# Moving the on-chip tiles of an attention and two-block MLP kernel to other byte positions within 128

## The chip, the cores and the metric

The kernel runs on one core of a Trainium2 chip. The time is the device time in microseconds of one execution; the time before is the median of three runs. A profile is one further execution, taken with the hardware profiler on.

In the profile PE is the matrix engine's matmuls, PEld its weight loads, DVE the vector engine, ACT the scalar engine, POOL the GpSimd engine and SP the engine whose queue issues all DMAs here.

## The reference

Three stages follow each other. Attention runs over 2 batches, 8 heads, 576 positions and a head width of 64; of each row of scores only the 32 largest count. Its output, 1152 rows of 512, goes through a first block (weights `moe_w_in` 512 x 2048 and `moe_w_out` 2048 x 512, Mish between them) and a second one of the same sizes with SiLU.

```python
scores = scale * np.matmul(q, k.transpose(0, 1, 3, 2))
kth = np.partition(scores, -top_k, axis=-1)[..., -top_k:-top_k + 1]
scores = np.where(scores >= kth, scores, -1e9)          # then softmax, then times v
h = x @ w_in;  g = h * np.tanh(softplus(h));  x = g @ w_out      # first block
h = x @ w_in;  g = h / (1 + np.exp(-h));      return g @ w_out   # second block
```

## The kernel before, in words

The 1152 rows are nine tiles of 128. `attention` (from line 356) works on one tile and one pair of heads at a time: scores on PE (line 391), copies to the tile `sc`, four rounds of finding and striking out the eight largest on DVE (lines 407 and 410), the exponential on ACT, transposes on PE (line 452, `e` against the identity matrix), the product with `v` (lines 468 and 471), and the result into the row tile `xt`.

`block1` (line 659) and `block2` (line 779) take the row tiles in groups, listed in `BLOCK1` and `BLOCK2`. A group marked `n` holds one 128-row tile (in the second block's first group two) and multiplies in plain fp32; each such matmul stands in the profile as two MATMUL records. A group marked `r` holds two tiles, 256 rows, and multiplies in the fp32r format: each operand is split into a high and a low part and three products are summed (`passes`, line 605), one record each. In the input products (line 644) the weights are the stationary operand, which PEld loads, and the rows (`xt` in the first block, `y` in the second) are the moving operand that streams through PE. In the first block's output product (line 714) the weights are stationary and the activations (`hs` in plain groups, `g` in split ones) move. In the second block's output product (line 821) it is the other way: `th` or `g` is stationary, and the weights move, 512 columns at a time. Weights lie in the tiles `wraw` (plain), `ws` (split) and `keep` (split, held for all groups).

The class `Plan` orders all steps by ranks and costs written in the tables at the top, and then emits them; each engine runs its instructions in that order.

All tiles in on-chip memory come from one pool, `sb`, through the helper `sbuf(tag, shape)`: a tag's first call reserves its buffers side by side, at the next multiple of 32 bytes of each partition. Tags follow each other in the order of their first calls, so a tile's length sets where the following ones lie. What this gives in the built program, as the byte position within 128 (the same in all 128 partitions, and for every slice that a matmul reads, since those slices begin at multiples of 128 bytes within their tiles):

| tiles | before |
|---|---|
| `ident` | 0 |
| `qraw`, `kraw` | 64 |
| `wide`, three buffers | 64, 96, 0 |
| `v`, `qs`, `kk`, `wraw`, `sc`, `ws`, `m8`, `rest` | 32 |
| `bias`, `den` (16 bytes each, at 32-byte steps) | all four |
| `e`, `x`, `pt`, `dt`, `xt`, `hs`, `y`, `th`, `g`, `o`, `keep` | 96 |

Of the kernel before, what the change touches and what calls it, by code (L numbers as in the profile page):

```python
# [10 lines left out]
F32 = mybir.dt.float32  # L11
F32R = mybir.dt.float32r
I32 = mybir.dt.int32
U32 = mybir.dt.uint32
I16 = mybir.dt.int16
# [5 lines left out]
P = 128  # L21
TOPK = 32
UNIT = 512
ONE16 = 2.0 ** 19
FAR = 2.0 ** 80
LOWEST = -3.0e38
# [46 lines left out]
class Plan:  # L73
# [13 lines left out]
    def add(self, ways, reads=(), writes=(), uses=(), rank=0.0, boost=0.0, table=None, load=0.0):  # L87

        first = rank - (boost if not isinstance(boost, str) else OFF[boost])
        offset = lambda o: o if not isinstance(o, str) else FLEX1[o] if rank < EARLY and o in FLEX1 else FLEX[o]
        ways = [(w[0], w[1], offset(w[2]), w[3], w[4] if len(w) > 4 else w[0] == "pool") for w in ways
                if offset(w[2]) is not None]
        self.steps.append(dict(ways=ways, reads=reads, writes=writes, uses=uses, rank=rank, first=first, table=table, load=load))
# [140 lines left out]
def act_us(n, psum=False):  # L237
    return (0.051 if psum else 0.093) + n * 0.000833


def dve_us(n):
    return 0.07 + n * 0.00104
# [6 lines left out]
def pool_us(n):  # L249
    return 0.18 + n * 0.0021  # L250
# [3 lines left out]
def kernel(ctx: ExitStack, tc, qh, kh, va, w1i, w1o, w2i, w2o, out):  # L254
# [11 lines left out]
    wide = {"w1i": w1i, "w1o": w1o, "w2i": w2i, "w2o": w2o}  # L266

    sb = ctx.enter_context(tc.tile_pool(name="sb", bufs=1))
    ps = ctx.enter_context(tc.tile_pool(name="ps", bufs=1, space=PSUM))
    dp = ctx.enter_context(tc.tile_pool(name="dp", bufs=1, space=DRAM))  # L270

    def sbuf(tag, shape, dtype=F32):
        return sb.tile(shape, dtype, tag=tag, name=tag, bufs=SBUF_BUFS.get(tag, KEEP))

    def psum(tag, shape):
        return ps.tile(shape, F32, tag="ps_" + tag, name="ps_" + tag, bufs=PSUM_BUFS[tag])
# [9 lines left out]
    def get(key, make):  # L286
        if key not in T:
            T[key] = make()
        return T[key]
# [18 lines left out]

    ident = sb.tile([P, P], F32, name="ident", bufs=1)
    make_identity(nc, ident)  # L310
    zone = sb.tile([P, 1], F32, name="zone", bufs=1)
    nc.gpsimd.memset(zone, -ONE16 * 14336)
    tiny = sb.tile([P, 1], F32, name="tiny", bufs=1)
    nc.gpsimd.memset(tiny, 1e-9)


# [2 lines left out]
    def load_kv(b, p, rank):  # L319
        if (b, p) in kv_done:  # L320
            return
        kv_done.add((b, p))
        kk, vv = ("kk", b, p), ("v", b, p)
        raw = ("kraw", b, p)
        first = b == 0 and p == 0
        for h in ([0], [1]) if first else ([0, 1],):
            hs = slice(h[0], h[-1] + 1)
            add([("sp", 0.06, 0, lambda hs=hs: nc.sync.dma_start(
                out=get(raw, lambda: sbuf("kraw", [P, 2, S]))[:, hs], in_=kh[b, p][:, hs]))],
                writes=[raw + (i,) for i in h], uses=[(raw, "kraw")], rank=rank - 8, boost="kload", load=len(h) * P * S * 4)  # L330
        for h in range(2):
            hi = lambda h=h: get(kk, lambda: sbuf("kk", [P, 2, S], F32R))[:, h]
            lo = lambda h=h: T[kk][D:, h]
            src = lambda h=h: T[raw][:, h]
            U = [(raw, "kraw"), (kk, "kk")]
            add(copy_ways(S, hi, src, dve="khi", twice=True), reads=[raw + (h,)], writes=[kk + (h, 0)], uses=U,
                rank=rank - 6, boost="k")
            add(tt_ways(S, lo, lambda h=h: T[raw][D:, h], lo, ALU.subtract, dve="klo"), reads=[raw + (h,), kk + (h, 0)], writes=[kk + (h, 1)],
                uses=U, rank=rank - 6, boost="k")
        add([("sp", 0.06, 0, lambda: nc.sync.dma_start(out=get(vv, lambda: sbuf("v", [P, NB + 1, D])), in_=va[b, p]))],  # L340
            writes=[vv], uses=[(vv, "v")], rank=rank, load=P * (NB + 1) * D * 4)
# [14 lines left out]
    def attention(t, p, rank):  # L356
# [8 lines left out]
        K = lambda name, *rest: (name,) + key + rest  # L365
# [36 lines left out]
        for i in range(TOPK // 8):  # L402
            for h in range(2):
# [5 lines left out]
                if i < TOPK // 8 - 1:  # L409
# [1 line left out]
                        out=rest()[:, h], in_to_replace=m8()[:, h, 8 * i:8 * i + 8], in_values=src()[:, h], imm_value=LOWEST))],  # L411
                        reads=srck + [K("m8", h, i)], writes=[K("rest", h)],
                        uses=srcu + [(K("rest"), "rest"), (K("m8"), "m8")] if i == 0 else srcu + [(K("m8"), "m8")], rank=rank)
        bias = lambda: get(K("bias"), lambda: sbuf("bias", [P, 2, 2, 1]))
        den = lambda: get(K("den"), lambda: sbuf("den", [P, 2, 2, 1]))
        for i, (col, by) in enumerate([(TOPK - 1, FAR), (0, -scale)]):
            if i == 0 and t < MASK:
                continue
# [86 lines left out]
    def convert(name, src, dst, rank, four):  # L505
        wk, sk, gk = ("w",) + name, ("pn",) + name, ("wide",) + name

        def fetch():
            t = get(gk, lambda: sbuf("wide", [P, 2 * UNIT + 2], I32)).bitcast(I16)[:, 1:1 + 4 * UNIT]
            s = src.bitcast(I16)  # L510
            if four:
                t = t.rearrange("p (f j) -> p f j", f=4)
            nc.sync.dma_start(out=t, in_=s)
        add([("sp", 0.06, 0, fetch)], writes=[gk], uses=[(gk, "wide")], rank=rank - 10, boost="cload", load=P * UNIT * 8)
        pn = lambda: get(sk, lambda: sbuf("ws", [P, 2, UNIT], I32))
        top = lambda: T[gk].bitcast(I16)[:, 4:4 + 4 * UNIT].rearrange("p (n t) -> p n t", t=4)[:, :, 0]
        mid = lambda: T[gk].bitcast(U32)[:, 1:1 + 2 * UNIT].rearrange("p (n t) -> p n t", t=2)[:, :, 0]
        for i in range(2):
            add([("act", act_us(UNIT) + 0.14, 0, lambda i=i: nc.scalar.activation(  # L519
                pn()[:, i], top(), AF.Relu, scale=ONE16 - 2 * ONE16 * i, bias=zone))],  # L520
                reads=[gk], writes=[sk + (i,)], uses=[(gk, "wide"), (sk, "ws")], rank=rank - 5, boost="cpn")
        se = lambda: pn()[:, 0]
        ways = [("pool", pool_us(UNIT), 0, lambda: nc.gpsimd.tensor_tensor(out=se(), in0=pn()[:, 0], in1=pn()[:, 1],  # L523
                                                                           op=ALU.subtract))]
        ways.append(("dve", dve_us(UNIT), "se", lambda: nc.vector.tensor_tensor(
            out=se(), in0=pn()[:, 0], in1=pn()[:, 1], op=ALU.subtract), True))
        add(ways, reads=[sk + (1,)], writes=[sk + (0,)], uses=[(sk, "ws")], rank=rank - 3, boost="cse")
        w = lambda: get(wk, lambda: sbuf("wraw", [P, UNIT]))
        T["conv"] = T.get("conv", 0) + 1
        if ADD and T["conv"] % ADD == 0:  # L530
            add([("act", act_us(UNIT) + 0.05, 0, lambda: nc.scalar.activation(w().bitcast(I32), mid(), AF.Copy, scale=2.0 ** -13))],  # L531
                reads=[gk], writes=[wk], uses=[(gk, "wide"), (wk, "wraw")], rank=rank - 5, boost="cmid")
            add([("pool", pool_us(UNIT), 0, lambda: nc.gpsimd.tensor_tensor(out=w().bitcast(I32), in0=w().bitcast(I32), in1=se(),  # L533
                                                                            op=ALU.add))],
                reads=[wk, sk + (0,)], writes=[wk], uses=[(sk, "ws"), (wk, "wraw")], rank=rank - 3, boost="cw")
        else:
            add([("dve", dve_us(UNIT), 0, lambda: nc.vector.scalar_tensor_tensor(
                out=w().bitcast(U32), in0=mid(), scalar=13, in1=se().bitcast(U32), op0=ALU.logical_shift_right,
                op1=ALU.bitwise_or), True)],
                reads=[gk, sk + (0,)], writes=[wk], uses=[(gk, "wide"), (sk, "ws"), (wk, "wraw")], rank=rank - 2, boost="cw")  # L540
        if not dst:
            return wk
        dk, dst_ap = dst
        add([("sp", 0.06, 0, lambda: nc.sync.dma_start(
            out=dst_ap(), in_=T[wk].rearrange("p (f j) -> p f j", f=4) if four else T[wk]))],
            reads=[wk], writes=[dk], uses=[(wk, "wraw")], rank=rank + 5, boost="wstore", load=P * UNIT * 4)
        return wk
# [292 lines left out]
    for t, (start, step) in enumerate(TILES):  # L840
        for p in range(NPAIR):
            attention(t, p, start + p * step)
# [52 lines left out]
```

## Time and profile before

| | us |
|---|---|
| median of three runs (lowest, highest) | 645.02 (644.46, 645.12) |
| the profiled execution's own time | 642.01 |
| its span, from the first to the last instruction | 640.2 |
| PE busy | 592.8 (93%) |
| DVE busy | 528.0 (82%) |
| ACT busy | 476.9 (74%) |
| POOL busy | 338.0 (53%) |

The profile's page gives the share of each engine, a picture in 40 slices of the span, the chain of work that ended last (each step followed back to what released it), and groups of like instructions with their mean duration. PE's matmuls overlap: a MATMUL record lasts some 280 ns while the next one starts after less than half of that. So the pace of PE is not read from a record's duration but from the chain, whose pieces give a time and a count of instructions that followed each other.

### The profile page before, as it was taken

To read this page: it belongs to the slowest core of one execution; us is meant where nothing else is said; L and a number is where in the kernel's file an instruction comes from. 1 tells how busy PE (TensorE), PEld (TensorE's weight loads), DVE (VectorE), ACT (ScalarE), POOL (GpSimd) and SP (SyncE) were. 2 spreads that over 40 slices of the span, in tenths; PEclk is the share of its full clock that TensorE was granted. 3 is DMA by queue.
4 is the path that set the end of the run, shared out by engine and by line. 5 is a ranking of instruction groups with operands and counts; after the bars stand their busy time and mean duration, and the time that the engine had idled before them with its cause. 6 is when DMAs were issued, how large, how long until landed. Compare 5 with 4: busy or idle time off the path is not lost.

```text
span 640.2 us, 13237 instructions
## 1 busy us (share of the span) xinstructions
PE 592.8 (93%) x4616; PEld 527.9 (82%) x4616; DVE 528.0 (82%) x1121; ACT 476.9 (74%) x991; POOL 338.0 (53%) x319
## 2 busy tenths in 40 slices
PE   1587739999999999999999999999999999999997
PEld 1476629999998966788999778999998999989986
DVE  4999999997999999789999989999996244755541
ACT  6899999897699999988997767996895344333321
POOL 6788886671367877877877426448782000000000
PEclk9998988999999999999999999999999999999999
DMA  9978886997798978999799697959669888887661
GB/s 307 298 226 275 278 251 208 341 335 233 237 326 267 309 247 264 302 370 357 266 383 369 219 341 275 317 164 343 223 221 346 329 306 307 284 253 266 238 193 70
DMA packets 85650, 178.34 MB, mean 279 GB/s; under 512 B 8144, under 2 KB 29136, under 8 KB 85584
## 3 DMA queue, kind: packets, MB, share of 16 engines
q1 hardware_dynamic: 85584, 177.50, 81.7%
q8 instruction: 36, 0.59, 0.4%
q14 instruction: 30, 0.25, 0.1%
HBM read 138.94 MB, written 38.54 MB: 277 GB/s over the span
## 4 chain that ended last, share of the span: by engine, by line
PE 73%; ACT 13%; DMA 7%; DVE 4%; POOL 1%; issue 1%; SPq 0%; POOLq 0%; ACTq 0%; DVEq 0%
PE ps_h L644 26%; PE ps_y L714 16%; PE ps_y L821 15%; PE ps_att L391 5%; PE ps_misc L468 5%; ACT ws L519 4%; PE ps_att L452 4%; DMA w2i<-wraw 2%; ACT wraw L531 2%; DVE m L407 2%; DMA wide<-in_w1o_dram 2%; DVE rest L410 2%; DMA qraw<-in_qh_dram 1%; ACT sc L295 1%; ACT pt L295 1%
## 5 line engine op out<-in xcount | busy, mean ns | idle before, releaser
L407 DVE MAX8 m<-rest 128x8 f32<-128x576 f32 x216 | 154.2, 745 | 0.1
L410 DVE MATCH_REPLACE8 rest<-m,rest 128x576 f32<-128x576 f32 x144 | 106.1, 741 | 0.0
L295 ACT CAST ws<-wraw 128x512 fp32r<-128x512 f32 x98 | 60.1, 622 | 55.8 <-PE ps_h L644 25.9
L519 ACT ACTIVATE ws<-wide,zone 128x512 int32<-128x512 int16 x128 | 95.2, 783 | 2.0 <-POOL wraw L533 1.3
L533 POOL TENSOR_TENSOR wraw<-wraw,ws 128x512 int32<-128x512 int32 x64 | 81.6, 1283 | 15.0 <-ACT wraw L531 3.1
L391 PE MATMUL ps_att<-kk,qs 128*128 128x288 f32 x320 | 67.7, 334 | 22.9 <-POOL kk L303 18.5
L523 POOL TENSOR_TENSOR ws<-ws 128x512 int32<-128x512 int32 x64 | 81.8, 1289 | 9.5 <-ACT ws L519 6.3
L303 POOL TENSOR_TENSOR ws<-wraw,ws 128x512 fp32r<-128x512 f32 x52 | 66.6, 1296 | 26.2 <-DVE ws L297 7.4
L391 PEld LDWEIGHTS ps_att<-kk,qs 128*128 128x128 f32 x320 | 49.1, 198 | 32.0 <-POOL kk L303 20.1
L644 PEld LDWEIGHTS ps_h<-y,ws 128*128 128x128 f32 x576 | 72.8, 188 | 3.0 <-issue 0.2
L644 PE MATMUL ps_h<-y,ws 128*128 128x256 f32 x576 | 75.0, 279 | 0.0
L644 PE MATMUL ps_h<-xt,ws 128*128 128x256 f32 x576 | 70.8, 279 | 0.0
L714 PE MATMUL ps_y<-g,ws 128*128 128x256 f32 x540 | 70.1, 280 | 0.0
L644 PEld LDWEIGHTS ps_h<-xt,ws 128*128 128x128 f32 x576 | 68.1, 188 | 0.8 <-issue 0.6
L305 DVE TENSOR_TENSOR ws<-wraw,ws 128x512 fp32r<-128x512 f32 x57 | 41.5, 734 | 30.2 <-ACT ws L295 29.8
L714 PEld LDWEIGHTS ps_y<-g,ws 128*128 128x128 f32 x540 | 65.3, 188 | 0.7 <-issue 0.7
L821 PE MATMUL ps_y<-ws,g 128*128 128x512 f32 x252 | 65.4, 398 | 0.0
L714 PE MATMUL ps_y<-hs,wraw 128*128 128x128 f32 x384 | 51.6, 282 | 7.6 <-ACT bias L419 7.6
L407 DVE MAX8 m<-sc 128x8 f32<-128x576 f32 x72 | 53.0, 746 | 4.2 <-ACT sc L295 4.1
L452 PE MATMUL ps_att<-ident,e 128*128 128x128 f32 x324 | 51.7, 286 | 3.9 <-DVE e L427 2.8
L714 PEld LDWEIGHTS ps_y<-hs,wraw 128*128 128x128 f32 x384 | 48.2, 198 | 8.3 <-POOL wraw L533 7.7
L410 DVE MATCH_REPLACE8 rest<-m,sc 128x576 f32<-128x576 f32 x72 | 53.1, 740 | 0.0
(90 smaller groups left out, 1147.7 us busy)
## 6 DMA issues: line engine op xcount, KB each, us to landing
wraw<-w1i SPq DMA_DIRECT2D x64, 256.0 KB, 4.5
wraw<-w2i SPq DMA_DIRECT2D x64, 256.0 KB, 3.9
ws<-w1o_split SPq DMA_DIRECT2D x30, 512.0 KB, 5.6
ws<-w2o_split SPq DMA_DIRECT2D x28, 512.0 KB, 4.6
wraw<-w1o SPq DMA_DIRECT2D x48, 256.0 KB, 4.9
wide<-in_w1i_dram SPq DMA_DIRECT2D x16, 512.0 KB, 5.6
wide<-in_w1o_dram SPq DMA_DIRECT2D x16, 512.0 KB, 5.0
wide<-in_w2i_dram SPq DMA_DIRECT2D x16, 512.0 KB, 4.8
```

The source lines that it names most:

```text
L295: ways.append(("act", act_us(n, psum), act, lambda: nc.scalar.copy(get_out(), get_in())))
L303: ways.append(("pool", pool_us(n), pool, lambda: nc.gpsimd.tensor_tensor(out=get_out(), in0=get_a(), in1=get_b(), op=op)))
L391: nc.tensor.matmul(o, lhsT=l, rhs=r[:, f * SH:(f + 1) * SH], start=(i == 0), stop=(i == len(ops) - 1))
L407: add([("dve", 0.67, 0, lambda i=i, h=h, src=src: nc.vector.max(out=m8()[:, h, 8 * i:8 * i + 8], in_=src()[:, h]))], reads=srck, writes=[K ...
L410: add([("dve", 0.73, 0, lambda i=i, h=h, src=src: nc.vector.match_replace(out=rest()[:, h], in_to_replace=m8()[:, h, 8 * i:8 * i + 8], in_ ...
L452: nc.tensor.transpose(o[:, i, :], ef[:, (c + i) * P:(c + i + 1) * P], ident)
L519: add([("act", act_us(UNIT) + 0.14, 0, lambda i=i: nc.scalar.activation(pn()[:, i], top(), AF.Relu, scale=ONE16 - 2 * ONE16 * i, bias=zone))],
L523: ways = [("pool", pool_us(UNIT), 0, lambda: nc.gpsimd.tensor_tensor(out=se(), in0=pn()[:, 0], in1=pn()[:, 1], op=ALU.subtract))]
L533: add([("pool", pool_us(UNIT), 0, lambda: nc.gpsimd.tensor_tensor(out=w().bitcast(I32), in0=w().bitcast(I32), in1=se(), op=ALU.add))], rea ...
L644: nc.tensor.matmul(hp[:, c, :], lhsT=l, rhs=rr, start=(i == 0), stop=(i == len(ops) - 1))
L714: nc.tensor.matmul(yp[:, o, :], lhsT=l[:, d * P:(d + 1) * P], rhs=rr[:, c, :], start=(fc == 0 and k == 0 and o == 0), stop=last, skip_grou ...
L821: nc.tensor.matmul(op, lhsT=gg[:, c, i * P:(i + 1) * P], rhs=wt, start=(fc == 0 and k == 0), stop=(fc == NFC - 1 and k == len(ops) - 1))
```

## The change

Every tile begins at a multiple of 128 bytes, except from `xt` on. Small tiles are given 32 words where they had 1 or 4, and `wide` 32 more words instead of 2. Ahead of the first `xt` tile an unused tile of 8 words (32 bytes) is reserved, and ahead of the first `y` tile one of 16 words (64 bytes), so that `xt` and `hs` lie at 32 and all after them at 96.

```diff
+ROOM = 32
+SHIFT = dict(xt=8, y=16)
...
     def sbuf(tag, shape, dtype=F32):
+        if tag in SHIFT:
+            get(("shift", tag), lambda: sb.tile([P, SHIFT[tag]], F32, name="shift_" + tag, bufs=1))
         return sb.tile(shape, dtype, tag=tag, name=tag, bufs=SBUF_BUFS.get(tag, KEEP))
+
+    def few(tag):
+        return sbuf(tag, [P, ROOM])[:, :4].rearrange("p (a b c) -> p a b c", a=2, b=2)
...
-    zone = sb.tile([P, 1], F32, name="zone", bufs=1)
+    zone = sb.tile([P, ROOM], F32, name="zone", bufs=1)[:, :1]
...
-    tiny = sb.tile([P, 1], F32, name="tiny", bufs=1)
+    tiny = sb.tile([P, ROOM], F32, name="tiny", bufs=1)[:, :1]
...
-        bias = lambda: get(K("bias"), lambda: sbuf("bias", [P, 2, 2, 1]))
-        den = lambda: get(K("den"), lambda: sbuf("den", [P, 2, 2, 1]))
+        bias = lambda: get(K("bias"), lambda: few("bias"))
+        den = lambda: get(K("den"), lambda: few("den"))
...
-            t = get(gk, lambda: sbuf("wide", [P, 2 * UNIT + 2], I32)).bitcast(I16)[:, 1:1 + 4 * UNIT]
+            t = get(gk, lambda: sbuf("wide", [P, 2 * UNIT + ROOM], I32)).bitcast(I16)[:, 1:1 + 4 * UNIT]
```

No instruction is added, removed or moved on any engine: each engine's instructions, their shapes and the semaphores they wait for stand in the same order as before, and only line numbers (7 more from `few` on) and addresses differ. What differs for a matmul is the distance from the moving operand's position to the stationary one's, within 128 bytes:

| matmul (line before): moving, stationary | before | after |
|---|---|---|
| 644 and 735: `xt`, `ws` or `wraw`; 714: `hs`, `wraw` | 64 | 96 |
| 644: `y`, `ws` or `wraw`; 714: `g`, `ws` | 64 | 32 |
| 821: `ws`, `g` or `wraw`, `th` | 64 | 96 |
| 714: `g`, `keep`; 821: `keep`, `g`; 391: `kk`, `qs` | 0 | 0 |
| 452: `ident`, `e`; 485: `ident`, `x` | 96 | 0 |
| 468 and 471: `pt`, `v` | 64 | 0 |

## Rows read from the trace of the kernel before

**Rows 1.** The page: its first lines, and the chain's shares by engine.

```profile
span 640.2 us, 13237 instructions
PE 592.8 (93%) x4616; PEld 527.9 (82%) x4616; DVE 528.0 (82%) x1121; ACT 476.9 (74%) x991; POOL 338.0 (53%) x319
...
PE 73%; ACT 13%; DMA 7%; DVE 4%; POOL 1%; issue 1%; SPq 0%; POOLq 0%; ACTq 0%; DVEq 0%
```

**Rows 2.** Busy time in three stretches: bounds, length, engines (instructions), clock, DMA.

```profile
0.00:290.00 290.00, 246.37 (x1928) 212.31 (x1928) 265.64 (x590) 262.46 (x537) 206.62 (x204) 0.98 0.86 283
290.00:480.00 190.00, 189.95 (x1567) 172.30 (x1567) 183.03 (x395) 158.50 (x360) 124.04 (x111) 1.00 0.82 289
480.00:640.20 160.20, 156.50 (x1125) 143.29 (x1124) 79.33 (x138) 55.92 (x96) 7.29 (x6) 1.00 0.75 259
```

**Rows 3.** The chain from 480 us on: start, us, what, count.

```profile
480.94 1.41 PE ps_h L644 x12
...
494.05 0.66 PE ps_att L452 x6
...
504.71 16.32 PE ps_h L644 x144
...
529.19 9.52 PE ps_y L714 x84
...
553.67 1.44 PE ps_y L714 x12
...
623.90 1.42 PE ps_h L644 x12
625.32 11.20 PE ps_y L821 x48
636.51 0.02 issue
```

**Rows 4.** The timeline of PE from 553.5 us: the instructions of one chain piece.

```profile
553.50 1.60 PE L714 MATMUL ps_y<-g,keep 128*128 128x256 f32 x12
```

**Rows 5.** The chain earlier on, plain fp32 matmuls.

```profile
137.75 3.57 PE ps_y L714 x32
...
243.32 1.73 PE ps_h L644 x8
...
394.50 0.86 PE ps_y L821 x2
```

**Rows 6.** PE's matmuls by operands from 480 us: count, busy us, mean ns.

```profile
L821 PE MATMUL ps_y<-ws,g 128*128 128x512 f32 x214 | 55.3, 397 | 0.0
L644 PE MATMUL ps_h<-y,ws 128*128 128x256 f32 x420 | 54.6, 279 | 0.0
L644 PE MATMUL ps_h<-xt,ws 128*128 128x256 f32 x192 | 22.6, 276 | 0.0
L714 PE MATMUL ps_y<-g,ws 128*128 128x256 f32 x180 | 21.9, 276 | 0.0
L821 PE MATMUL ps_y<-keep,g 128*128 128x512 f32 x36 | 9.3, 394 | 0.0
...
L714 PE MATMUL ps_y<-g,keep 128*128 128x256 f32 x12 | 1.6, 283 | 0.0
```

**Rows 7.** The same from 290 to 480 us.

```profile
L714 PE MATMUL ps_y<-g,ws 128*128 128x256 f32 x360 | 48.3, 283 | 0.0
L644 PE MATMUL ps_h<-xt,ws 128*128 128x256 f32 x337 | 41.8, 279 | 0.0
...
L644 PE MATMUL ps_h<-y,ws 128*128 128x256 f32 x156 | 20.5, 281 | 0.0
L452 PE MATMUL ps_att<-ident,e 128*128 128x128 f32 x126 | 18.7, 274 | 0.0
```

**Rows 8.** The tile `wide`, all three buffers: ACT's duration in ns, min/median/max.

```profile
L519 ACT ACTIVATE ws<-wide,zone x128: 738/776/888, 8.6 to 293.4; 128x512 int32<-128x512 int16 x128
```

## The prediction

> **What bounds the kernel now.** I read the page's engine line and chain first, then the three stretches of busy time, then the chain piece by piece from 480 us on, and last PE's matmuls by operands. The page shows PE as the busiest engine and the chain on PE for 73% of the span [rows 1]. The stretches show where that is strict [rows 2]. Before 290 us PE is busy 246 of 290 us and DVE 266: a mixed stretch, in which a faster matmul mostly waits for something else. From 290 to 480 us PE is busy for all but 0.05 of 190 us, but DVE has work for 183.0 of them, so that only 190.0 - 183.0 = 7.0 us could be saved there before DVE's row of top-32 searches is the limit. From 480 us PE alone is busy; the chain runs over nothing but PE from there to 636.5 us [rows 3]. Time saved per matmul there is saved in full.
>
> So the question is whether the pace of a matmul depends on where its operands lie. The chain gives paces [rows 3]. 256-column fp32r matmuls go at two of them: 16.32 us for 144 and 9.52 us for 84, both 113.3 ns each; and 1.41 or 1.42 us for 12, about 117.6 ns. The slow piece occurs 28 times from 480 us (first at 480.94, last at 623.90): 336 matmuls. 512-column ones take 11.20 us for 48, 233.3 ns each. One more piece of 12 takes 1.44 us, 120 ns each; the timeline names its operands as `g` and `keep` [rows 4]. That is the one group of 256 columns whose two operands lie at distance 0; the others are at distance 64.
>
> Plain fp32 streams at half that rate and shows what the same columns cost with less pressure on the memory [rows 5]: the piece of 8 at 243.32 us (256 columns, `y` against `wraw`) takes 216 ns each, and that of 2 at 394.50 us (512 columns) 430 ns. Half of these, 108 ns and 215 ns, I take as the floor of the fp32r matmuls. Above it stand 113.3 - 108 = 5.3 ns and 117.6 - 108 = 9.6 ns for 256 columns, and 233.3 - 215 = 18.3 ns for 512. I read this excess as PE's two streams, the moving operand and the next weights, getting in each other's way. The row of `keep` supports it: with another position of the stationary operand alone, 120 ns.
>
> **The change part by part.** It adds, removes and moves no instruction, so every term is a pace.
>
> *From 480 us.* There are 420 + 192 + 180 + 12 = 804 matmuls of 256 columns and 214 + 36 = 250 of 512 [rows 6]. Excess: 336 x 9.6 ns = 3.2 us, 468 x 5.3 ns = 2.5 us, 250 x 18.3 ns = 4.6 us; 10.3 us together, all on the path.
>
> *From 290 to 480 us.* 360 + 337 + 156 = 853 of 256 columns, with mean durations of 279 to 283 ns [rows 7] where the slow pace goes with 279 and the fast one with 276 [rows 6]; so the slow pace, 853 x 9.6 ns = 8.2 us of excess. DVE lets at most 7.0 us of it through.
>
> *Distances 32 and 96.* After the change nearly all these matmuls have one of them; no fp32r row of before does, so the gain is bounded from both sides. All the excess may go (-10.3 and -7.0 us), or it may rise to the 120 ns of `keep` or above (below, rival 3). The nearest row inside is that of the transposes, `ident` against `e`, at distance 96 and half rate: 0.66 us for 6, 110 ns [rows 3]. Plain matmuls of the same 128 columns at distance 64 take 3.57 us for 32, 111.6 ns [rows 5]. Above the 108 ns floor that is 2.0 instead of 3.6 ns, about half. I take half for the fp32r matmuls too: -5.1 us from 480 us; -4.1 us of the 8.2 before, of which I let half through, -2.0 us, since DVE has hardly any slack and PE's order is fixed.
>
> *Before 290 us.* The plain matmuls there may lose 1.6 ns each by the same rule; a few hundred of them make under 1 us, in a stretch that other engines share. I count -0.3 us.
>
> *What gets worse.* The transposes go from distance 96 to 0. If they then take the 111.6 ns, 126 from 290 to 480 us [rows 7] cost 126 x 1.6 ns = 0.2 us. The products of `pt` and `v` go from 64 to 0, and no row shows a difference between these two at half rate: 0, at most 0.3 us either way.
>
> *The other engines.* ACT reads `wide` from three buffers at 64, 96 and 0, and its 128 reads keep to a median of 776 ns between 738 and 888 [rows 8]; I cost every edit off PE at nothing, bounded by 0.5 us, since PE covers them from 290 us on. The unused tiles have no instruction.
>
> *Sum.* -5.1 - 2.0 - 0.3 + 0.2 = -7.2, say -7 us. Against the profiled execution, 642.0 us (its span of 640.2 and 1.8 around it), that is 635.0. The median of the runs is 3.0 us above that execution, so I forecast 645.0 - 7.0 = 638.0 us.
>
> **The rivals.**
>
> 1. *All the excess goes.* For it: 108 ns is what the half-rate pieces allow. Against it: two paces at one and the same distance show that the position is not the only thing that sets the pace. 10.3 + 7.0 = 17.3 us off, 627.7 us.
>
> 2. *Nothing changes.* For it: the same distance of 64 gives 113.3 ns in one stretch and 117.6 in another, so the pace may hang on what went before (a run keeps the pace that it began with), and the step to 120 ns rests on a few pieces of 12. Then 645.0 us, give or take the 0.3 us of the transposes. The Trainium skill, in "SBUF — State Buffer", section "Who interferes with whom", speaks for this one: PE reads moving operand and weights through two independent ports and "PE and ACT never wait on anyone", so positions should not matter. Here the trace does not bear it out as far as it goes: 113.3, 117.6 and 120 ns for the same instruction.
>
> 3. *Slower: 32 and 96 are as bad as 0.* The mechanism: with the full-rate stream passing twice as many bytes as the weights, what counts may be that the two are half the 128 bytes apart, and the old 64 would be the best of the four distances; the move to 32 and 96 then gives that up in lines 644, 714 and 821, most of all after 480 us. For it: 64 is better than 0 in the only fp32r pair of rows [rows 3, 4]. Against it: the half-rate transposes do better at 96 than the others at 64. Price: all 256-column matmuls at 120 ns are 336 x 2.4 + 468 x 6.7 ns = 3.9 us from 480 us and 853 x 2.4 ns = 2.0 us before, paid in full, since PE has no idle time there. For 512 columns `keep` and `ws` have mean durations of 394 and 397 ns [rows 6], so anything from 0 to the same growth as at 256 columns (3.9 on 5.7, or two thirds of 4.6 us: 3.1 us). Together 5.9 to 9.0 us: 651 to 654 us. It decides from the point where the new pace of the `y` matmuls is above 117.6 ns.
>
> **How the numbers follow.** Half the excess or somewhat less or more: 0.44, with a range of its own from 634 to 642 us. All of it: 0.13. Nothing: 0.18. Slower: 0.25. The measurement can tell 0.2%, some 1.3 us, from no change. Faster by more than that: the first two, 0.57; within it: 0.18; slower: 0.25. The range reaches from between the first two cases to the lower side of the slow one: 630 to 651 us; outside stay the full gain and the worse half of rival 3.
>
> **What would show it.** The pieces of line 644 (651 after) from 555 us, now 12 in 1.41 us: at 1.33 to 1.37 us the forecast holds, at 1.30 rival 1, at 1.44 or more rival 3. The last 48 matmuls of line 821 (828 after): 11.20 us now; 10.7 us or less in the forecast. The transposes: 0.66 us for 6, no less than that. DVE should be busy for more than 96% of its stretch from 290 us up to the end of the top-32 searches, and have its last search no more than 3 us earlier. The sums by engine of DVE, ACT and POOL should stay within 1%; if one of them moves more, I mis-costed the tiles off PE. The forecast is wrong if the paces change and the time does not, or if the time changes where PE is not the bound.

## The result, and the profile after

The changed kernel takes 651.43 us (median of 14 runs, 647.59 to 655.47), against 645.64 us for the kernel before in 14 runs beside it. The ratio is 1.0085, 95% interval 1.0061 to 1.0108: slower, by some 5.5 us (0.0085 x 645.64). The prediction said 638 us and 630 to 651: the wrong direction, and the time just above the range. The profiled execution took 652.46 us.

The page's first lines and the chain's shares, which answer to [rows 1]:

```profile
span 650.7 us, 13237 instructions
...
PE 602.2 (93%) x4616; PEld 537.4 (83%) x4616; DVE 527.7 (81%) x1121; ACT 477.6 (73%) x991; POOL 337.5 (52%) x319
...
PE 66%; ACT 16%; DMA 10%; DVE 4%; POOL 2%; issue 2%; SPq 0%; ACTq 0%; POOLq 0%; DVEq 0%
```

Only PE and its weight loads became busier, by 9.4 and 9.5 us; DVE, ACT and POOL did the same work in the same time to within 0.7 us. The three stretches, with bounds moved so that each holds the same instructions as in [rows 2] to within two per engine (bounds, length, then busy time and count of PE, PEld, DVE, ACT, POOL; granted clock, DMA share, GB/s):

```profile
0.00:295.50 295.50, 251.19 (x1928) 216.38 (x1930) 265.11 (x590) 262.40 (x536) 206.24 (x204) 0.95 0.85 277
295.50:487.40 191.90, 191.44 (x1566) 174.38 (x1567) 183.22 (x395) 159.28 (x361) 123.99 (x111) 1.00 0.83 287
487.40:650.70 163.30, 159.55 (x1126) 146.61 (x1124) 79.38 (x138) 55.92 (x96) 7.27 (x6) 1.00 0.76 254
```

The second stretch grew by 1.9 us and the third by 3.1 us, both with PE busy nearly throughout. The first grew by 5.5 us in this pair of profiles, at a granted clock of 0.95 against 0.98; the experiments show below that this part is mostly not the change's.

The chain of after (start, us, what, count), with pieces that answer to [rows 3 to 5], two plain fp32 ones first:

```profile
142.65 3.57 PE ps_y L721 x32
...
217.72 1.73 PE ps_h L651 x8
...
486.29 0.66 PE ps_att L459 x6
...
512.13 16.80 PE ps_h L651 x144
...
537.49 10.08 PE ps_y L721 x84
...
564.83 2.87 PE ps_h L651 x24
...
622.94 1.44 PE ps_h L651 x12
...
635.73 11.24 PE ps_y L828 x48
```

The 144 matmuls on `xt` (distance 96 now) went from 113.3 to 116.7 ns each, the 84 on `g` (32) from 113.3 to 120.0, the twelves on `y` (32) from 117.6 to 119 to 120. The 48 of 512 columns stayed at 234 ns (233 before), the transposes at 110 ns though their distance went from 96 to 0, the plain matmuls at 111.6 and 216 ns though theirs went from 64 to 96 or 32.

The same matmuls by operands, over the last stretch (from 487.5 us: count, busy us, mean ns), against [rows 6]:

```profile
L651 PE MATMUL ps_h<-y,ws 128*128 128x256 f32 x420 | 55.8, 282 | 0.0
L828 PE MATMUL ps_y<-ws,g 128*128 128x512 f32 x214 | 55.2, 398 | 0.0
L651 PE MATMUL ps_h<-xt,ws 128*128 128x256 f32 x192 | 23.3, 279 | 0.0
L721 PE MATMUL ps_y<-g,ws 128*128 128x256 f32 x180 | 23.0, 282 | 0.0
```

The three rows of 256 columns gained 3 to 6 ns in mean duration, the 512-column row 1. Off PE, `wide` reads as before [rows 8], now with all three buffers at 0:

```profile
L526 ACT ACTIVATE ws<-wide,zone x128: 743/774/848, 8.7 to 298.9; 128x512 int32<-128x512 int16 x128
```

### The profile page after: what moved, and what is told of

It reads as the page before. It is cut to its first block, busy times and chain, and to the rows that moved or that the text cites. A ratio compares the mean times of both kernels' runs of the same rounds, so it can differ in the third digit from the quotient of the medians.

```text
span 650.7 us, 13237 instructions
## 1 busy us (share of the span) xinstructions
PE 602.2 (93%) x4616; PEld 537.4 (83%) x4616; DVE 527.7 (81%) x1121; ACT 477.6 (73%) x991; POOL 337.5 (52%) x319
## 4 chain that ended last, share of the span: by engine, by line
PE 66%; ACT 16%; DMA 10%; DVE 4%; POOL 2%; issue 2%; SPq 0%; ACTq 0%; POOLq 0%; DVEq 0%
PE ps_h L651 23%; PE ps_y L721 16%; PE ps_y L828 13%; ACT ws L526 5%; PE ps_att L398 4%; PE ps_misc L475 4%; PE ps_att L459 3%; ACT wraw L538 2%; DMA wide<-in_w2i_dram 2%; DMA w2i<-wraw 2%; DVE m L414 1%; ACT pt L302 1%; ACT e L430 1%; DMA wide<-in_w1o_dram 1%; ACT sc L302 1%
## 5 line engine op out<-in xcount | busy, mean ns | idle before, releaser
L398 PE MATMUL ps_att<-kk,qs 128*128 128x288 f32 x320 | 69.8, 342 | 23.4 <-POOL kk L310 19.1
L398 PEld LDWEIGHTS ps_att<-kk,qs 128*128 128x128 f32 x320 | 50.8, 205 | 33.2 <-POOL kk L310 20.9
L651 PEld LDWEIGHTS ps_h<-y,ws 128*128 128x128 f32 x576 | 74.3, 188 | 3.0 <-issue 0.2
L651 PE MATMUL ps_h<-y,ws 128*128 128x256 f32 x576 | 76.8, 282 | 0.0
L721 PE MATMUL ps_y<-g,ws 128*128 128x256 f32 x540 | 72.4, 284 | 0.0
L721 PEld LDWEIGHTS ps_y<-g,ws 128*128 128x128 f32 x540 | 67.3, 188 | 0.7 <-issue 0.7
```

The lines of the kernel that those rows point to most:

```text
L398: nc.tensor.matmul(o, lhsT=l, rhs=r[:, f * SH:(f + 1) * SH], start=(i == 0), stop=(i == len(ops) - 1))
L651: nc.tensor.matmul(hp[:, c, :], lhsT=l, rhs=rr, start=(i == 0), stop=(i == len(ops) - 1))
L721: nc.tensor.matmul(yp[:, o, :], lhsT=l[:, d * P:(d + 1) * P], rhs=rr[:, c, :], start=(fc == 0 and k == 0 and o == 0), stop=last, skip_grou ...
```

## The experiments

Theory: the pace of a 256-column fp32r matmul depends on the distance of its two operands within 128 bytes; 64 is good, 96 a little worse, 32 and 0 bad. Rivals: absolute positions count; tiles off PE count; the transposes' operands count.

For all full kernels I use one more number, worked out from the trace: the time from the start of the 2001st matmul record (299 us before, 305 after) to the start of the last one. PE bounds nearly all of it, so it shows a change of pace without what happens earlier. Added up by operands from start to start, the 4.7 us that this stretch has more in after's profile than in the first one of before are 1.7 for `y` against `ws`, 2.1 for `g` against `ws`, 1.2 for `xt` against `ws`, and -0.4 for all else.

| kernel | distance of `xt`; `y`, `g` | ratio to before (95%) | from matmul 2001, us |
|---|---|---|---|
| before, two profiles | 64; 64 | | 337.3, 337.5 |
| after | 96; 32 | 1.0085 (1.0061 to 1.0108) | 342.0 |
| all 64 | 64; 64 | 1.0024 (1.0003 to 1.0045) | 339.5 |
| all 0 | 0; 0 | 1.0059 (1.0034 to 1.0084) | 342.3 |
| all 32 | 96; 96 | 1.0028 (1.0003 to 1.0053) | 338.8 |
| before, 32 up | 64; 64 | 1.0010 (0.9983 to 1.0037) | 337.4 |
| distance 16 | 16; 16 | 1.0003 (0.9976 to 1.0030) | 337.7 |
| distance 48 | 48; 48 | 1.0071 (1.0041 to 1.0101) | 341.7 |
| `xt` 256 up | 64; 64 | 1.0033 (1.0003 to 1.0063) | 337.6 |
| all 64, `e` at 96 | 64; 64 | 1.0038 (1.0017 to 1.0059) | 338.0 |
| all 64, `ident` at 96 | 64; 64 | 1.0007 (0.9981 to 1.0032) | 337.4 |
| before, `ident` apart | 64; 64 | 1.0022 (1.0000 to 1.0044) | 337.7 |

The last column lies within 337.3 to 337.7 us in all kernels whose paces are those of before. Ratios repeat less well: four kernels with these paces (the two moved up, and the last two) measured 1.0007 to 1.0033. So a ratio up to about 1.0035 alone is not read as an effect here.

**All at distance 64.** The changed kernel with only its shifts edited: every tile at multiples of 128 bytes, and from `xt` on at 64.

```diff
-SHIFT = dict(xt=8, y=16)
+SHIFT = dict(xt=16)
```

> The changed kernel with the distance of before: all tiles at multiples of 128, but the unused tile ahead of xt is 16 words and the one ahead of y is gone, so that xt, hs, y, th, g, o and keep all lie at 64 and every product of rows or activations with ws or wraw is at distance 64, as before. Theory A (the distance within 128 bytes between PE's two operands sets its pace): 256-column fp32r matmuls at 113.3 and 117.6 ns again, none of ws at 120; time that of before within 0.3%. Theory B (it is the tiles off PE, or the multiples of 128 themselves, that cost): 116.7 to 120 ns as in the changed kernel and 0.6 to 1.1% slower than before. Theory C (most of the loss is the early stretch, up to 126 us, where the changed kernel's profile fell 4.9 us behind): paces as before and still 0.5% or more slower.

```profile
508.33 1.37 PE ps_y L828 x6
509.70 16.96 PE ps_h L651 x144
...
535.14 9.89 PE ps_y L721 x84
```

The `y` and `g` matmuls are back from 120 to 117.7 ns, and 2.5 of the 4.6 us that after has above before in the last column are back too. But the long runs go at 117.7 ns, where before ran at 113.3: at distance 64 there are two paces, and this kernel falls into the other one. At its slow pace 64 is no better than the 116.7 ns that `xt` has at 96. So the distance explains part of it, and something else picks between the two paces of 64.

**All at 0.**

```diff
-SHIFT = dict(xt=8, y=16)
+SHIFT = dict()
```

> The changed kernel without either unused tile: every tile at a multiple of 128, all distances 0. Theory A: the pace that g against keep had before, 120 ns, for all 256-column fp32r matmuls, also those of xt, which in the changed kernel went at 116.7; 600 matmuls of xt at 3 ns more make it about 2 us slower than the changed kernel, 1.1 to 1.4% slower than before. Theory B: as the changed kernel, 0.6 to 1.1% slower than before. Theory C: the same as the changed kernel.

```profile
511.00 17.27 PE ps_h L651 x144
...
536.92 10.08 PE ps_y L721 x84
...
634.84 10.92 PE ps_y L828 x48
```

119 to 120 ns for the 256-column matmuls from 511 us on, as `keep` had shown [rows 4], while the last 48 of 512 columns are quicker, 227.5 ns. The pace came as expected by theory A, the time did not: 1.1 to 1.4% above before was expected and 0.59% came, and the last column is that of after. From matmul 2001 on the `xt` matmuls cost 1.4 us more than in after, those of `ws` against `g` 0.6 us less.

**All at 32.** The change without its second unused tile: `xt` keeps its new distance of 96, and `y` and `g` have 96 too instead of 32.

```diff
-SHIFT = dict(xt=8, y=16)
+SHIFT = dict(xt=8)
```

> The changed kernel without the unused tile ahead of y: xt, hs, y, th, g, o and keep at 32. Products with ws or wraw as the stationary operand are at distance 96, as those of xt were in the changed kernel; the second block's output product is at 32 instead of 96. Theory A: 116.7 ns for all 256-column fp32r matmuls, y's and g's too (119.7 in the changed kernel), so some 1100 x 3 ns = 3 us faster than the changed kernel, 0.3 to 0.5% slower than before; the 512-column matmuls stay at 233 ns. If the pace is set by which tile it is and not by the distance, y and g stay at 119.7 ns and the time is that of the changed kernel.

```profile
510.88 16.80 PE ps_h L651 x144
...
536.08 9.80 PE ps_y L721 x84
```

Both go at 116.7 ns. Of the 4.6 us that the change costs in the last column, 1.4 are there already; the other 3.2 come with the second unused tile, which puts `y` and `g` at distance 32. (That tile also sets the distance of the second block's output product, 32 here and 96 in after; its last 48 matmuls take 233.5 and 234 ns.)

**Before, all tiles 32 bytes up.**

```diff
+    sb.tile([P, 8], F32, name="ahead", bufs=1)
     ident = sb.tile([P, P], F32, name="ident", bufs=1)
```

> The kernel before with an unused tile of 32 bytes reserved ahead of all others: every position moves by 32, every distance stays. Theory A: the time of before within 0.3%, paces 113.3 and 117.6 ns. If the position itself counts and not the distance between two operands, other paces, and a time that differs.

```profile
509.80 16.32 PE ps_h L645 x144
...
534.27 9.52 PE ps_y L715 x84
```

Every position is another one and every distance the same, and so are paces and time. As far as a move of 32 bytes can tell, positions as such do not count.

**The paces by themselves.** A kernel of its own, which leaves out the whole computation of the reference: for each position of the moving tile 24 matmuls of 256 columns (`first`), 12 of 512 (`long`), 24 of 256 again (`again`), three passes over the operands as in the kernel; the letters are the shift in words (a is 0, j is 9), and the distance is minus four times it. `narrow` has 32 stationary columns instead of 128.

```python
def run(name, n, off, count, m=P):
    t = ps.tile([m, n], F32, tag=f"p{n}", name="ps_" + name, bufs=2)
    for i in range(count):
        k, j = i // 3 * 2 + (i % 3 == 2), i // 3 + (i % 3 == 1) * 2
        a = off + 512 * (j % 3) if n == 512 else off + 256 * (j % 7)
        nc.tensor.matmul(t, lhsT=wt[:, 128 * (k % 16):128 * (k % 16) + m], rhs=xt[:, a:a + n], start=(i == 0), stop=(i == count - 1))
    ...
```

> A kernel of its own that leaves out the whole reference computation and writes a partial product in its place: runs of fp32r matmuls as in the split groups (24 of 256 columns, 12 of 512, 24 of 256 again), all against the same stationary tile, with the moving operand moved in steps of 8 bytes through 128 bytes, and then on by 128 to 448 bytes; at the end four distances with only 32 stationary columns. Theory A (distance within 128 bytes): at 64 paces of 113 or 118 ns, at 96 about 117, at 0 and 32 about 120, the same again 128 bytes further on; 512 columns at 231 to 235 ns everywhere; with 32 stationary columns instead of 128 the excess over 108 ns falls, since a quarter of the weights is read. If the distance is not what counts but the tiles' absolute places or what the other engines do, all distances go alike. A distance that no kernel here has had (between the multiples of 32) may be below 113 ns.

The chain, with distances 0, 96, 56, 32, 16, 8, then 64 with the shift of 192 bytes, then `narrow` at 0 and 96:

```profile
21.17 2.87 PE ps_againaaa L41 x24
...
55.16 2.80 PE ps_againaai L41 x24
...
97.60 2.93 PE ps_againabi L41 x24
...
123.24 2.88 PE ps_againace L41 x24
...
140.21 2.72 PE ps_againaci L41 x24
...
148.67 2.92 PE ps_againada L41 x24
...
160.06 2.83 PE ps_firstaei L41 x24
...
165.69 2.73 PE ps_againaei L41 x24
...
201.97 2.72 PE ps_narrowaaa L41 x24
...
207.46 2.82 PE ps_narrowaai L41 x24
```

In this order 119.7, 116.7, 121.9, 119.9, 113.3 and 121.6 ns. At distance 64 the same 24 matmuls took 117.8 ns the first time and 113.6 the second: both paces within 8 us and at the same addresses. None of the 22 shifts went below 113.3 ns, and the 512-column runs kept to 229 to 236 ns at all of them. So it is shown without the rest of the kernel that the pace goes with the distance; 64 stands first, with 16, only at its quick pace, and at its slow one it lies behind 96 (117) and 112 (116.7 to 117). Of the narrow runs distance 0 gained most (113.4 ns), 32 went from 119.9 to 117.2 and 64 from 117.8 to 116.7, and 96 did not gain (117.5). The theory that the load of the next weights causes it would want narrow weights to help everywhere, and is not shown.

**Before, once more,** unchanged: would the two paces fall elsewhere in another execution?

> The kernel before, unchanged, once more. If the two paces of 113 and 118 ns come from the program and its positions, the same stretches are fast and slow as in the first profile (144 matmuls of line 644 at 113.3 ns near 505 us, the pieces from 555 us at 117.6 ns) and the time from the 600th matmul to the last is again 514.9 us within 0.5 us. If chance sets them, other stretches. The stretch up to the 600th matmul, 121.3 us in the first profile and 126.2 us in the changed kernel's, shows how much of that 4.9 us is chance.

```profile
507.52 16.32 PE ps_h L644 x144
...
532.00 9.52 PE ps_y L714 x84
```

The long runs have the same paces, and so has every piece of 256 columns from 480 us on. Earlier that does not hold: of the 107 pieces of at least 12 such matmuls against `ws` in the whole profile, 9, all between 296 and 446 us, have 113 ns in one execution and 118 in the other. So the program does not pick the pace by itself; before 480 us an execution can pick it too. The 601st matmul began 121.3 us into the first profile of before, 123.7 into this one, 125.9 into that of before with all tiles 32 up and 126.2 into that of after. So most of the 4.9 us that after's profile had lost by then come without any change of pace.

**Distance 16.** The kernel before with `xt`, `y` and `g` 48 bytes further on inside larger tiles.

```diff
+MOVE = 12
...
+    def moved(tag, shape, dtype=F32):
+        n = int(np.prod(shape[1:]))
+        t = sbuf(tag, [P, n + 32], dtype)[:, MOVE:MOVE + n]
```

> The kernel before with xt, y and g moved by 48 bytes inside longer tiles (position 16), so that the weights stand at distance 16 from the moving rows and activations (64 before). Theory A with the paces of the kernel of runs (distance 16: 115.4 and 113.3 ns): all 256-column fp32r matmuls of xt, y and g at 113.3 to 115.4 ns, where before had 114.9 (xt), 117.1 (y) and 115.3 (g); from the 600th matmul to the last 512 to 515 us (515.1 before), so 0 to 0.5% faster than before. If the paces in a lone stream of matmuls do not carry over to the full kernel, 117 ns or more and slower.

```profile
509.71 16.34 PE ps_h L652 x144
...
534.49 9.80 PE ps_y L722 x84
```

113.5 and 116.7 ns, of which the second is above the 115.4 that was expected: as good as 64, not better. No gain was found.

**Distance 48.** The same with `MOVE = 4`.

> The kernel before with xt, y and g moved by 16 bytes (position 112): distance 48. Theory A with the kernel of runs (118.4 and 118.2 ns there): the 256-column fp32r matmuls of xt, y and g at 118 ns on average; some 1450 of them at 2.6 ns more than before make 3 to 4 us, 0.4 to 0.7% slower than before. If only multiples of 32 bytes count, or the parity of 32-byte pieces, the pace of distance 32 or 64: 119.7 ns, or 113.3 and 117.6.

```profile
511.50 17.28 PE ps_h L652 x144
...
537.33 9.99 PE ps_y L722 x84
```

120.0 and 118.9 ns, and slower by 0.71%: a distance that the change does not use, taken from the run of paces (118.2 to 118.4 ns there), costs as much as the change. The direction of the forecast from that run held, the pace was 0.5 to 2 ns worse.

**`xt` 256 bytes up** in the kernel before: other addresses, same distances within 128.

```diff
+SHIFT = dict(xt=64)
...
+        if tag in SHIFT:
+            get(("shift", tag), lambda: sb.tile([P, SHIFT[tag]], F32, name="shift_" + tag, bufs=1))
```

> The kernel before with an unused tile of 256 bytes ahead of xt: xt and all after it 256 bytes further on, every distance within 128 bytes as before. It asks why the first study's kernel at distance 64 throughout took the slower of the two paces more often (xt 116.9 ns on average, 114.9 before; 518.0 us from the 600th matmul to the last, 515.1 before). If 128 bytes are the whole period: paces and time of before (xt 114.9, y 117.1, g 115.3 ns; 515 us). If the period is 256 or 512 bytes: xt near 116.9 ns, 517 to 518 us, 0.3 to 0.5% slower than before.

```profile
510.19 16.32 PE ps_h L647 x144
```

Paces of before. Its ratio of 1.0033 is not explained by them: the profile has the excess ahead of matmul 2001.

**All at 64, with `e`, `x`, `pt` and `dt` at 96** as before, so that the transposes have their old distance.

```diff
-SHIFT = dict(xt=16)
+SHIFT = dict(e=24, xt=24)
```

> The changed kernel with xt and all after it at distance 64 from the weights, and with e, x, pt and dt at 96 again, so that transposes and products with v have the distances that they had before (96; for v it is 96 instead of 64). If a run of fp32r matmuls takes over its pace from what ran ahead of it, and the transposes' and v's distances set that: xt back near 114.9 ns and 515 us from the 600th matmul to the last, time of before within 0.3%. If the period is longer than 128 bytes: 116.9 ns and 518 us again, as in the kernel at distance 64 throughout.

```profile
508.19 16.96 PE ps_h L651 x144
...
533.63 9.89 PE ps_y L721 x84
...
567.49 1.39 PE ps_h L651 x12
568.88 1.37 PE ps_y L828 x6
```

In the long runs the slow one of the two paces stays; the transposes' distance alone does not pick it. Behind them, from 565 us on, 21 of the 24 twelves on `y` take 115.2 to 115.7 ns each and most sixes of 512 columns 228.8, where all at 64 had 117.8 and 233.4: one more pair of paces at the same distances. It is worth 1.4 us, and so the last column reads 338.0 and not 339.5.

**All at 64, with the identity matrix at 96.**

```diff
+    sb.tile([P, 24], F32, name="ahead", bufs=1)
     ident = sb.tile([P, P], F32, name="ident", bufs=1)
+    sb.tile([P, 8], F32, name="behind", bufs=1)
```

> As the run with all operands at distance 64, but with the identity matrix at position 96, so that in the transposes the moving operand stands to the weights of the matmuls that follow as it did before (identity 0, weights 32: distance 96), where that run had 0. Theory A (which of the two paces of distance 64 a run of matmuls takes is set by the step from the transposes to the matmuls behind them): the 144 matmuls on xt after 480 us take 16.3 us (113.3 ns each), the stretch around them 51.8 us as before, and the time is that of before within 0.2%. Theory B (the pace is picked by something else, such as the positions themselves): 16.9 to 17.0 us for the 144 (117.7 ns), and 0.2 to 0.5% slower than before.

```profile
511.67 16.32 PE ps_h L653 x144
...
536.15 9.52 PE ps_y L723 x84
```

Theory A's numbers: 113.3 ns in both runs, 337.4 us from matmul 2001, the time of before. With this and distance 64, all that the change had cost is back, though every large tile still lies at other positions than before, and the small tiles and `wide` have their new room: the tiles off PE cost nothing that can be seen.

**Before, with only the identity matrix moved against the rest,** the converse.

```diff
     ident = sb.tile([P, P], F32, name="ident", bufs=1)
+    sb.tile([P, 24], F32, name="behind", bufs=1)
```

> The kernel before with an unused tile of 96 bytes behind the identity matrix: every tile after it moves by 96 bytes, so that all matmuls of weights with rows and activations keep their distance of 64, and only the identity matrix stands otherwise to the rest (identity and weights both at 0; before 0 and 32). Theory A (the step from the transposes to the matmuls behind them sets which of the two paces of distance 64 is taken): the 144 matmuls on xt after 480 us go from 16.32 to about 16.96 us, the 84 of the output product from 9.52 to 9.89, and the time is 0.1 to 0.5% above before. Theory B (the identity's place has no part in it): 16.32 and 9.52 us, and the time of before within 0.2%.

```profile
508.82 16.32 PE ps_h L645 x144
...
533.30 9.52 PE ps_y L715 x84
```

Theory B's numbers: identity and weights both at 0 as in the run of all at 64, and yet 113.3 ns. So the step from the transposes to the matmuls is not what picks the pace, and theory A falls. Whether the identity's move to 96 brought the quick pace in the preceding experiment is not shown either: that kernel was profiled once, and all tiles behind the identity lay 128 bytes further on than in all at 64.

**Where the choice falls.** The traces at distance 64 (before twice, 32 up, `xt` up, identity apart, and the three of all at 64) show this much. In each of the eight profiles 24 pieces of 256 columns against `ws` directly follow another such piece, and all 24 have the pace of the one ahead. So the 432 matmuls that begin with the 144 have one pace. They take 48.96 us in six profiles and 50.88 us in two, all at 64 and all at 64 with `e` at 96. The first of them takes its pace on behind six 512-column matmuls on `keep`, whose own time goes with it; in the kernel before, ahead of the 144 of [rows 3], they stand as

```profile
503.31 1.40 PE ps_y L821 x6
```

and in all at 64 as the 1.37 us shown above. The 1.9 us between 48.96 and 50.88 are nearly all of the 2.1 us that all at 64 has above before in the last column: one choice, made once, and not a distance measured many times over. What makes it stays open.

## Why the prediction was wrong

*PE as the bound: right.* (From 480 us DVE and ACT work too, 79 and 56 us [rows 2]; what holds is that the chain runs on PE.) From 290 us a slower matmul cost its full price: 1.9 and 3.1 us in the two stretches, and the 4.6 us from matmul 2001 on (342.0 - 337.4) are 0.71% of 645.6 us, of the 0.85% measured. The small rest, and the first stretch, cannot be told from what varies there without the change.

*The pace depends on the distance: right, and shown.* At 0, 32 and 96 the kernels' long runs have 119.9, 120.0 and 116.7 ns and the kernel of runs has 118.2 to 119.7, 119.7 to 119.9 and 116.7 to 117.0, and moving everything together by 32 bytes changes no pace of a long run. It does not depend on the distance alone: 64 has 113.3 and 117.8 ns. Of the 4.6 us the 3.2 between `y` and `g` at 96 and at 32 stand clear of the choice between these two; the 1.4 that are there with all three at 96 are counted against a kernel that has the quick one in its long runs.

*The floor of 108 and 215 ns: wrong.* I halved the plain fp32 paces [rows 5] and called what stands above it excess that a position could remove. No position gave less than 113.3 ns at 256 columns, which the kernel before already had in its long runs. At 512 columns, where I put the largest part of the excess (4.6 of 10.3 us), none of the distances in the kernel brought the gain that I wanted: the last 48 took 233 to 234 ns each at 64, 96 and 32, 232 at 80, 230 at 112 (where the runs called 48 and 16 put this product) and 228 at 0, at most 6 of the 18.3 ns. Two kinds of matmul do not give each other's floor.

*Half of it goes at 32 and 96: wrong, and this is the step that turned the sign.* It rested on one pair of rows, transposes at distance 96 with 110 ns [rows 3] against plain matmuls at 64 with 111.6 ns [rows 5]. The pair differs in kind as well as in distance, and the kind was the cause: after the change the transposes stand at 0 and still take 110 ns, and the plain matmuls stand at 96 and still take 111.6. The distance has no effect on either, so this pair could tell nothing of fp32r. The pair that was of one kind, fp32r at 64 and at 0 with 113.3 or 117.6 against 120 ns [rows 3, 4], pointed the other way; I gave it to rival 3.

*All slow from 290 to 480 us: misread,* with little effect on the forecast. The mean durations of 279 to 283 ns [rows 7] hide both paces: from start to start, 339 of the intervals there lie at 112 to 115 ns and 468 at 116 to 119, by which the excess was 339 x 5.3 + 468 x 9.6 ns = 6.3 us and not 8.2.

*Rival 3 was the case.* Its mechanism (64 the best of the four distances, at its quick pace) and its mark (12 matmuls in 1.44 us) hold: 1.43 to 1.44. Its price was 3.9 us from 480 us and 2.0 before (339 x 6.7 + 468 x 2.4 ns = 3.4 by the paces that the earlier stretch really had); measured are 3.1 and 1.9, less because `xt` at 96 goes at 117 ns and not at 120. Its 0 to 3.1 us for 512 columns turned out nothing. Its reason, two streams half of 128 bytes apart, is not shown: 16 is as good as 64.

*Rival 2* was refuted, but for its remark that a run keeps the pace that it began with, which the traces at distance 64 bear out. The rule that I named with it, of the Trainium skill, "SBUF — State Buffer", section "Who interferes with whom", would leave the pace alone if it covers PE's own two streams, as I took it; the runs show 113.3 to 122 ns by distance, and the measurement decides. Which part of PE or of the memory does the waiting, no run here shows.

*Edits off PE at nothing, the transposes, `pt` and `v`, the plain matmuls:* right to cost at little. The sums of DVE, ACT and POOL stayed within 0.2%, and none of the named pieces moved.

## What to carry to other kernels

Read a suspected effect of one variable from rows that differ in that variable alone: one fp32r pair here outweighed a tidier pair of two kinds. In a kernel bound by fp32r matmuls of 256 columns, the byte distance within 128 between moving and stationary tiles is worth up to 6% of the pace (113.3 against 120 ns), so an unused tile ahead of one of them is a cheap trial, and moving tiles for any other reason needs the paces read again. A long run of one pace is one observation of it, not as many as it has matmuls: look at what stands ahead of it, too. Judge such a change by a stretch that PE bounds: there it repeated to 0.4 us, where ratios of whole runs strayed by 0.3%.

## What the runs showed of the hardware that was not expected

- Paces of 256-column fp32r matmuls by distance, in ns: 16 and 64 have two, 113.3 to 115.7 and 116.7 to 118.5; 96 has 117; 48 and 80 have 116.7 to 120; 0 and 32 have 118 to 121; 8 and 56 up to 122. At 512 columns 228 to 236 at the distances seen; plain fp32 and transposes at 128 columns 111.6 and 110 at both distances seen.
- Two paces at one distance. A piece takes over that of the 256-column piece directly ahead of it (24 of 24 in each of eight profiles), so 432 matmuls can hang on one choice (48.96 or 50.88 us). Two executions of the kernel before made the same choices from 480 us on, and differed in 9 pieces of 107 before that. What picks stays open.
- No version was found that beats the kernel before; distance 16 equals it at 1.0003 (0.9976 to 1.0030).
